# A fused decode backward kernel: outer products in two-row-group pieces under a scheduled TensorE order, in place of four-row-group units in a written order

## The chip, the cores and the metric

The kernel runs on one core of one Trainium2 chip. The metric is the time of one execution on the device, in microseconds. Three runs of the kernel before took 589.41, 590.72 and 583.35 us; their median is 589.41 us. The engines are named as in the profile: PE (TensorE, matmuls), PEld (TensorE's weight loads), DVE (VectorE), ACT (ScalarE), POOL (GpSimd, which also issues the store transfers), SP (SyncE, which issues the load transfers).

## The reference

One token for each of two batch entries passes a layer norm, and the normed row feeds two branches whose outputs are added to the input: attention over a cache, and a gated MLP. The kernel computes the output and the gradients of everything but a second, unused input.

```python
xn  = layernorm(x)                                   # x: 2 x 1 x 576, bf16
q   = (xn @ wq).reshape(2, 1, 32, 128)               # 32 query heads, 16 cache heads
s   = einsum(q, k_cache) * 128 ** -0.5               # caches: 2 x 16 x 4096 x 128
p   = softmax(s);  o = einsum(p, v_cache)            # two query heads share a cache head
out = x + o.reshape(2, 1, 4096) @ wo + ((xn @ w_gate) * (xn @ w_up)) @ w_down   # width 4608
grads = vjp(out)(grad_out)   # of x, k_cache, v_cache, wq, wo, w_gate, w_up, w_down
```

The gradients of the two caches have the caches' size. Each is an outer product per cache head: a column of probabilities (or of score gradients) times a row of 128. So 92.48 MB are read and 92.48 MB are written.

## The kernel before

**Iterations.** The 16 cache heads form 4 groups of 4. An iteration takes one group, one batch entry and two heads: 16 iterations (`NIT`), four to a group. In each, two K heads and two V heads (1 MB each, `head_load`) come in on SP's queue.

**Scores.** `head_scores` (L499 to L514) turns half a head with DVE transposes of 32 x 32 blocks (L104, tile X) and multiplies it with a stationary tile W in 16 matmuls of 128 columns (L510), summed in one PSUM tile ps_sc. K heads give the scores, V heads the gradients of the probabilities. It is a generator: it stops after eight matmuls, so that other work can be put between.

**Softmax.** `softmax_units` (L569 to L608) gives three pieces, called in steps j = 4, 5 and 6 of the iteration, among the V scores. `dscores` (L610) makes the score gradients in the next iteration. `masked` (L540) lets GpSimd spread rows with a mask into prm and dsm, the left operands of the outer products.

**Contractions.** `contract` (L516, 64 matmuls of 32 columns of weights) multiplies the rows with V (for the output) at j = 0 of the next iteration, and with K (for the gradient of q) at j = 2; `select` follows one step later. Until then the heads hold their slots in the ring `nat` of 12 slots, which also holds the weights wq, wo (of a group) and wgu, wd (of an MLP slice).

**Outer products.** `outer_units` (L547) gives four units for two heads. A unit takes both PSUM buffers ps_o, of two banks each, and fills them with 16 matmuls in which the row group a runs fastest:

```python
o = [ps_o(), ps_o()]
for c in range(4):
    for a in range(4):
        nc.tensor.matmul(o[a // 2][:, a % 2, c * Dh:(c + 1) * Dh],
                         lhsT=rows[32 * a:32 * a + 32, 4 * ch + c, :], ...)
```

Then `evac` (L86) copies each buffer to a store tile of 8 KB a partition; it picks ACT (L95) or DVE (L92) by a planned load of the two, which it adds up while the program is written. After two units GpSimd issues the store of the whole head (L564, 1 MB). The store tiles come from a ring `st` of five. The MLP's and the weights' gradients (`outer_gu`, `outer_down`, `outer_tail`, `outer_q`, `outer_qt`, `outer_o`) have the same form; in the last group the tiles of wq's and wo's gradients come from `nat`.

**Order.** TensorE's instructions stay in the order in which they are written (`manual_schedule`, L83); the other engines' order is found by the scheduler. The main loop (L812 to L886) has eight steps j an iteration: eight score matmuls, one outer unit (`more`), eight score matmuls, then pieces of the previous iteration's contractions, of the softmax, and of `side`, the list of other work (`other`). An MLP slice (one of nine, 512 wide, `mlp_units`) is loaded at j = 3 of iterations 0, 1, 2, 4, 6, 8, 10 and 12 and its ten units join `side` at the next iteration; slice 0 is there at the start. The next group's weights are loaded at the third iteration of a group. After the last iteration one more round of the loop issues the eight outer units that are left, and behind it come the last group's `back_units` and the final rows.

Of the kernel before, what the change touches and what calls it, by code (L numbers as in the profile page):

```python
# [13 lines left out]
P = 128  # L14
# [9 lines left out]
def kernel(  # L24
# [30 lines left out]
    G = 4  # L55
# [26 lines left out]

    ctx.enter_context(tc.manual_schedule(engines={mybir.EngineType.PE}))  # L83
# [178 lines left out]
    def dxn(stat, weight, pos, koff, kstep, half):  # L262


        Wm, Wt = stat
        X = xtile([P, 9, FS // 2], "Xw")
        t32(view(pairs(X[:].rearrange("p c n -> p (c n)")), 0, P, 0, [[1, 9 * P]]),
            view(pairs(weight[:].rearrange("p c n -> p (c n)")), 0, P, P * half, [[2 * P, 9], [1, P]]))
        dve(1.4)
        dp = ps_m([P, 160])  # L270
        for r in range(4):
            for gq in range(4):
                q, s = 2 * half + gq // 2, 4 * (gq % 2) + r
                nc.tensor.matmul(  # L274
                    dp[32 * gq:32 * gq + 32, 0:P], lhsT=view(Wm[:], 0, P, 8 * pos(q, s), [[1, 32]]),
                    rhs=view(X[:], 0, P, koff(s) * 256 + (2 * (q % 2) + (s // 2) % 2) * 64 + s % 2,
                             [[kstep * 256, 4], [2, 32]]),
                    start=(r == 0), stop=(r == 3))
        for r in range(2):
            for gq in range(4):  # L280
                q, s = 2 * half + gq // 2, 2 * (gq % 2) + r
                nc.tensor.matmul(
                    dp[32 * gq:32 * gq + 32, P:160], lhsT=view(Wt[:], 0, P, 8 * (4 * q + s), [[1, 32]]),
                    rhs=view(X[:], 0, P, 8 * 256 + (2 * (q % 2) + s // 2) * 64 + s % 2, [[2, 32]]),
                    start=(r == 0), stop=(r == 1))
        nc.vector.tensor_add(accx[:], accx[:], dp[:])
        dve(0.35)


    def mlp_units(i):  # L290
# [62 lines left out]
        def back(half):  # L353
            return lambda: dxn(m["W"], m["wgu"], lambda q, s: q * 8 + s, lambda s: (s // 4) * 4, 1, half)

        def outer_gu(w):
            def f():
                hb = m["hb"]
                st = swtile([P, 4, FS], "stw")
                o = [ps_o(), ps_o()]  # L360
                for dc in range(4):
                    for a in range(4):
                        nc.tensor.matmul(o[a // 2][:, a % 2, dc * P:(dc + 1) * P],
                                         lhsT=xnr[32 * a:32 * a + 32, dc * P:(dc + 1) * P],
                                         rhs=hb[32 * a:32 * a + 32, 1 + w, :], start=True, stop=True)
                for A in range(2):
                    evac(view(st[:], 0, P, 256 * A, [[P, 2], [FS, 4], [1, P]]),
                         o[A][:].rearrange("p a (d f) -> p a d f", d=4), 1024)
                out = (out_6, out_7)[w]
                nc.gpsimd.dma_start(out[0:512, f0:f0 + FS].rearrange("(c p) n -> p c n", p=P), st[:])  # L370
            return f

        def outer_tail():
            hb = m["hb"]
            st = tailtile("stt")
            o = [ps_o(), ps_o()]
            for w in range(2):
                for a in range(4):
                    nc.tensor.matmul(o[a // 2][64 * w:64 * w + 64, a % 2, 0:P], lhsT=xnr[32 * a:32 * a + 32, 512:576],
                                     rhs=hb[32 * a:32 * a + 32, 1 + w, :], start=True, stop=True)  # L380
            for A in range(2):
                evac(st[:, 256 * A:256 * A + 256].rearrange("p (a f) -> p a f", a=2), o[A][:, :, 0:P], 256)
            for w, out in enumerate((out_6, out_7)):
                nc.gpsimd.dma_start(out[512:576, f0:f0 + FS], st[64 * w:64 * w + 64])

        def outer_down(k):
            def f():
                hb = m["hb"]
                if k == 0:
                    m["sd"] = swtile([P, FC, D], "std")  # L390
                st = m["sd"]
                o = [ps_o(), ps_o()]
                for a in range(4):
                    nc.tensor.matmul(o[a // 2][:, a % 2, 0:HD2], lhsT=hb[32 * a:32 * a + 32, 0, :],  # L394
                                     rhs=dyr[32 * a:32 * a + 32, k * HD2:(k + 1) * HD2], start=True, stop=True)
                for A in range(2):
                    evac(st[:, 2 * A:2 * A + 2, k * HD2:(k + 1) * HD2], o[A][:, :, 0:HD2], D)
                if k == 1:
                    nc.gpsimd.dma_start(out_8[f0:f0 + FS, :].rearrange("(a p) n -> p a n", p=P), st[:])
            return f  # L400

        loads()
        return [gate_up, down, grads, outer_down(0), outer_down(1), back(0), back(1), outer_gu(0), outer_gu(1), outer_tail]


# [12 lines left out]
    def front_units(g, wq, wo):  # L418
        qd = sb.tile([P, 3, GH, 2], BF16, tag="qd", bufs=2, name="qd")
        rep = sb.tile([P, 2, 4, GH * 2], BF16, tag="rep", bufs=2, name="rep")  # L420

        def query():
            qp = ps_m([P, GH, 2])
            for h in range(GH):
                for dc in range(5):
                    if dc < 4:
                        l, r = wq[:, 2 * dc + h // 4, (h % 4) * P:(h % 4 + 1) * P], xs[:, dc, 0:2]
                    else:
                        l, r = wq[:, 8, (h % 4) * P:(h % 4 + 1) * P], xs[:, 4 + h // 4, 0:2]
                    nc.tensor.matmul(qp[:, h, :], lhsT=l, rhs=r, start=(dc == 0), stop=(dc == 4))  # L430
            nc.vector.tensor_copy(qd[:, 0], qp[:])
            nc.vector.tensor_scalar(qd[:, 2], qd[:, 0], SCALE, None, op0=ALU.mult)

        def grad(half):
            def f():
                Xo = xtile([P, GH // 2, D], "Xo")
                t32(pairs(Xo[:].rearrange("p c n -> p (c n)")),
                    pairs(wo[:, 4 * half:4 * half + 4].rearrange("p c n -> p (c n)")))
                do_ps = ps_m([P, P])
                for k in range(NB):  # L440
                    for e in range(2):
                        nc.tensor.matmul(
                            do_ps[:], lhsT=Wdy[:, k, e, :], rhs=view(Xo[:], 0, P, 64 * k + e, [[D, 4], [2, 32]]),
                            start=(k == 0 and e == 0), stop=(k == NB - 1 and e == 1),
                        )
                dof = sb.tile([P, GH // 2, 32], FP32, tag="dof", bufs=2, name="dof")
                t32(dof[:].rearrange("p c n -> p (c n)"), do_ps[:])
                nc.vector.tensor_copy(qd[:, 1, 4 * half:4 * half + 4], dof[:, :, 0:2])
                dve(2.0)
            return f  # L450

        def spread(t):

            def f():
                rp = ps_m([P, 4, GH * 2])
                for be in range(4):
                    nc.tensor.matmul(rp[:, be, :], lhsT=sel[:, be].rearrange("p a i -> p (a i)"),
                                     rhs=qd[:, t].rearrange("p h b -> p (h b)"), start=True, stop=True)
                nc.vector.tensor_copy(rep[:, t], rp[:])
            return f  # L460

        st = dict(g=g, wq=wq, wo=wo, qd=qd, rep=rep, oT=oTs[g % 2])
        return st, [query, grad(0), spread(0), grad(1), spread(1)]
# [35 lines left out]
    def head_scores(n, t, x, s_ps, half):  # L499
# [5 lines left out]
        for e in range(2):  # L505
            if e == 1:
                yield
# [8 lines left out]
    def contract(rowsT, heads):  # L516
# [13 lines left out]
        o_sb = sb.tile([P, Dh], FP32, tag="o_sb", bufs=2, name="o_sb")  # L530
        nc.scalar.copy(o_sb[:], o_ps[:])
        act(0.3)
        return o_sb

    def select(o_sb):
# [11 lines left out]
    def outer_units(rows, bd, b, l0, oview):  # L547
        m = {}

        def unit(x, ch):  # L550
            def f():
                if ch == 0:
                    m["st"] = stile([P, 4, 8, Dh], "so")
                st = m["st"]
                o = [ps_o(), ps_o()]
                for c in range(4):
                    for a in range(4):
                        nc.tensor.matmul(o[a // 2][:, a % 2, c * Dh:(c + 1) * Dh],  # L558
                                         lhsT=rows[32 * a:32 * a + 32, 4 * ch + c, :],
                                         rhs=bd[32 * a:32 * a + 32, x * Dh:(x + 1) * Dh], start=True, stop=True)  # L560
                for A in range(2):
                    evac(st[:, 2 * A:2 * A + 2, 4 * ch:4 * ch + 4, :].rearrange("p a c d -> p a (c d)"), o[A][:], 1024)
                if ch == 1:
# [3 lines left out]
        return [unit(x, ch) for x in range(2) for ch in range(2)]  # L567

    def softmax_units(s_ps, r):  # L569
        def largest():  # L570
            mx = small("mx")
            nc.vector.reduce_max(mx[:], s_ps[:], axis=AX.X)
            mT = ps_m([1, P])
            nc.tensor.transpose(mT[:], mx[:], identf[:])
            m4 = small("m4", (1, 4))
# [230 lines left out]
    for f in front:  # L806
        f()
# [112 lines left out]
```

## Time and profile before

| | |
|---|---|
| profiled execution, its own time | 589.41 us |
| its span, first to last instruction | 587.6 us |
| mean granted TensorE clock | 0.745 |
| read and written | 92.48 MB each, 315 GB/s over the span |
| loads (SP's queue) and stores (GpSimd's queue), share of the 16 DMA engines' span | 42.8% and 41.9% |
| one eviction of a ps_o buffer, 128 x 1024, on ACT / on DVE | 1.015 / 1.220 us |
| one X transpose on DVE | 1.230 us |
| one mask on GpSimd | 1.888 us |
| store of one head, issue to landing (median) | 7.7 us |
| load of one K / V head, issue to landing (median) | 9.0 / 9.5 us |

In a group's row, "out<-in xcount" is followed by the group's busy time in us and the mean of one in ns, then by the idle time of the engine just before them and what ended most of it. A row of waits reads: engine, what it wrote, what it waited for, the line of that; us in total, times, the longest. PEclk is the share of full speed that TensorE's clock was granted. Matmuls are pipelined, so one matmul's duration includes the way through the array, and the distance between starts tells the rate.

### The profile page before, as it was taken

To read this page: it belongs to the slowest core of one execution; us is meant where nothing else is said; L and a number is where in the kernel's file an instruction comes from. 1 tells how busy PE (TensorE), PEld (TensorE's weight loads), DVE (VectorE), ACT (ScalarE), POOL (GpSimd) and SP (SyncE) were. 2 spreads that over 40 slices of the span, in tenths; PEclk is the share of its full clock that TensorE was granted. 3 is DMA by queue.
4 is the path that set the end of the run, shared out by engine and by line. 5 is a ranking of instruction groups with operands and counts; after the bars stand their busy time and mean duration, and the time that the engine had idled before them with its cause. 6 is when DMAs were issued, how large, how long until landed. Compare 5 with 4: busy or idle time off the path is not lost. (4 is left out here: it accounts for less than half of the span.)

```text
span 587.6 us, 20030 instructions
## 1 busy us (share of the span) xinstructions
PE 447.7 (76%) x8921; PEld 351.1 (60%) x8921; DVE 360.5 (61%) x636; ACT 332.1 (57%) x454; POOL 204.5 (35%) x372
## 2 busy tenths in 40 slices
PE   0677897696787888887888878877887878878763
PEld 0576675474666666666666656666676656656630
DVE  8685543565465555667665656567665646679555
ACT  1036666464575655665665756655666756676644
POOL 5115242141242342524242442524242443442412
PEclk9987757676677558769876667779878677799655
DMA  8985969779589799997989899897979899975554
GB/s 269 387 304 188 358 237 392 288 264 364 209 280 394 291 327 405 335 410 290 365 280 407 327 333 395 317 402 265 375 270 405 343 363 398 327 306 214 217 218 162
DMA packets 52911, 186.26 MB, mean 317 GB/s; under 512 B 4140, under 2 KB 19128, under 8 KB 44632
## 3 DMA queue, kind: packets, MB, share of 16 engines
q1 hardware_dynamic: 28392, 92.49, 42.8%
q0 software_dynamic: 24432, 92.48, 41.9%
q8 instruction: 70, 1.15, 0.8%
q14 instruction: 17, 0.14, 0.1%
HBM read 92.48 MB, written 92.48 MB: 315 GB/s over the span
## 5 line engine op out<-in xcount | busy, mean ns | idle before, releaser
L95 ACT CAST so<-ps_o 128x1024 bf16<-128x1024 f32 x232 | 224.6, 1015 | 152.7 <-PE ps_o L558 97.5
L104 DVE STREAM_TRANSPOSE X<-kv 128x1024 f32<-128x1024 f32 x128 | 156.5, 1230 | 100.0 <-PE ps_sc L510 56.4
L510 PE MATMUL ps_sc<-X,W 128*128 128x128 bf16 x2048 | 205.9, 259 | 11.3 <-DVE X L104 11.3
L510 PEld LDWEIGHTS <-W 128*128 128x128 bf16 x2048 | 155.6, 114 | 41.3 <-issue 29.7
L564 POOL DMA_DIRECT2D out_dram<-so x64 | 49.4, 772 | 90.7 <-ACT so L95 61.3
L558 PE MATMUL ps_o<-bd,prm 32*128 32x128 bf16 x1024 | 36.7, 252 | 32.3 <-ACT stw L95 13.0
L558 PE MATMUL ps_o<-bd,dsm 32*128 32x128 bf16 x1024 | 40.3, 265 | 11.8 <-ACT so L95 7.6
L558 PEld LDWEIGHTS <-prm 32*128 32x128 bf16 x1024 | 21.7, 105 | 43.9 <-issue 29.3
L525 PE MATMUL ps_m<-kv,rowT 128*32 128x128 bf16 x2048 | 47.1, 264 | 0.0
L543 POOL TENSOR_TENSOR dsm<-ds,maskc 128x1024 bf16<-128x1024 bf16 x16 | 30.2, 1888 | 34.0 <-DVE ds L622 34.0
L525 PEld LDWEIGHTS <-rowT 128*32 128x32 bf16 x2048 | 40.2, 120 | 3.0 <-issue 2.4
L479 POOL COPY dM<-qd 128x128 bf16<-128x128 bf16 x32 | 9.2, 289 | 92.9 <-PE ps_m L485 81.6
L92 DVE CAST so<-ps_o 128x1024 bf16<-128x1024 f32 x24 | 29.3, 1220 | 19.8 <-PE ps_o L558 17.5
L558 PEld LDWEIGHTS <-dsm 32*128 32x128 bf16 x1024 | 22.9, 110 | 25.3 <-issue 21.3
L472 POOL COPY W<-rep 32x16 bf16<-32x16 bf16 x128 | 24.6, 192 | 36.7 <-PE ps_sc L510 26.8
L543 POOL TENSOR_TENSOR prm<-pr,maskc 128x1024 bf16<-128x1024 bf16 x16 | 30.2, 1888 | 20.5 <-DVE pr L600 20.5
L95 ACT CAST stw<-ps_o 128x1024 bf16<-128x1024 f32 x29 | 28.2, 1015 | 9.0 <-ACT so L95 4.2
L104 DVE STREAM_TRANSPOSE Xw<-wgu 128x1152 f32<-128x1152 f32 x18 | 24.7, 1370 | 9.9 <-PE ps_sc L510 9.9
L370 POOL DMA_DIRECT2D out_dram<-stw x18 | 13.7, 760 | 37.1 <-ACT stw L95 21.1
L95 ACT CAST sto<-ps_o 128x576 bf16<-128x576 f32 x27 | 16.7, 645 | 14.1 <-PE ps_o L705 12.6
L95 ACT CAST std<-ps_o 128x576 bf16<-128x576 f32 x35 | 21.7, 659 | 3.4 <-PE ps_o L394 3.4
L257 POOL COPY Wt<-Wm 64x128 bf16<-64x128 bf16 x26 | 7.4, 285 | 40.4 <-DVE mr L578 24.3
(179 smaller groups left out, 577.7 us busy)
## 6 DMA issues: line engine op xcount, KB each, us to landing
out_dram<-so POOLq DMA_DIRECT2D x64, 1024.0 KB, 7.7
kv<-in_A_k_cache_dram SPq DMA_DIRECT2D x32, 1024.0 KB, 9.0
kv<-in_A_v_cache_dram SPq DMA_DIRECT2D x32, 1024.0 KB, 9.5
out_dram<-stw POOLq DMA_DIRECT2D x18, 512.0 KB, 9.4
wd<-in_B_w_down_dram SPq DMA_DIRECT2D x9, 576.0 KB, 6.1
out_dram<-std POOLq DMA_DIRECT2D x9, 576.0 KB, 4.8
wo<-in_A_wo_dram SPq DMA_DIRECT2D x4, 1152.0 KB, 15.2
wgu<-in_B_w_gate_dram SPq DMA_DIRECT2D x9, 512.0 KB, 7.2
```

The costliest lines, as they stand in the source:

```text
L92: nc.vector.tensor_copy(out=out, in_=in_)
L95: nc.scalar.copy(out, in_)
L104: nc.vector.transpose(out, in_)
L257: nc.gpsimd.tensor_copy(view(Wt[:], 64 * h, 64, 0, [[P // n, n], [1, P // n]]), view(Wm[:], 64 * h, 64, off, dims))
L370: nc.gpsimd.dma_start(out[0:512, f0:f0 + FS].rearrange("(c p) n -> p c n", p=P), st[:])
L472: nc.gpsimd.tensor_copy(view(W[t][:], 32 * a, 32, 28 + 32 * a, [[2 * WW, 4], [WW + 2, 2], [1, 2]]), view(st["rep"][:], 32 * a, 32, t * 4 * ...
L479: nc.gpsimd.tensor_copy(view(dM[:], 0, P, t * 2 * P, [[P + 2, 2], [4, 32], [1, 2]]), view(st["qd"][:], 0, P, (2 if t == 0 else 1) * GH * 2 ...
L510: nc.tensor.matmul(s_ps[:], lhsT=view(W[t][:], 0, P, (be * 2 + x) * WW + 28 - 4 * c8, [[1, P]]), rhs=view(X[:], 0, P, c8 * 64 + e, [[8 * 6 ...
L525: nc.tensor.matmul(o_ps[32 * cg:32 * cg + 32, :], lhsT=view(rowsT[:], 0, P, c4 * 32 + 4 * c8, [[1, 32]]), rhs=head[:, 8 * c4 + c8, :], sta ...
L543: nc.gpsimd.tensor_tensor(m[:], view(rows[:], 0, P, 0, [[0, 8], [1, P]]), view(maskc[:], 0, P, 0, [[1, 8], [0, P]]), ALU.mult)
L558: nc.tensor.matmul(o[a // 2][:, a % 2, c * Dh:(c + 1) * Dh], lhsT=rows[32 * a:32 * a + 32, 4 * ch + c, :], rhs=bd[32 * a:32 * a + 32, x * ...
L564: nc.gpsimd.dma_start(oview[b, :, :, l0 + x].rearrange("a m n -> m a n"), st[:].rearrange("p a c d -> p a (c d)"))
```

## The change

It does the following:

- `manual_schedule` goes: the scheduler finds TensorE's order too.
- Every outer product is cut in two pieces. A piece takes one ps_o buffer and two of the four row groups: eight matmuls, one eviction. `more` issues two pieces where it issued one unit. A store tile is still filled by four evictions, and a store still covers one head.
- The pieces of the softmax, of the front part of a group and of `contract` / `select` become one function each, called in one go. K scores, softmax, V scores and `dscores` lie in one iteration. V is contracted at its end; K is contracted in the middle of the next iteration's first head.
- `side` is a list of lists of pieces; `other` issues a list at a time, as many as leave it empty after four head slots. An MLP slice joins whenever fewer than five entries are left, its loads first. By the built program slices lie in iterations 0 to 8.
- The next group's weights are loaded at the fourth iteration of a group, not at the third.
- All tiles of gradients come from the ring `st`, in the last group too; `o_sb` and `dof` have one buffer in place of two.
- After the loop, outer pieces and back part are issued in turn, the final rows ahead of the last weights' gradients.

The core of the diff:

```diff
-    ctx.enter_context(tc.manual_schedule(engines={mybir.EngineType.PE}))
...
     def head_scores(n, t, x, s_ps, half):
...
         for e in range(2):
-            if e == 1:
-                yield
...
-        o_sb = sb.tile([P, Dh], FP32, tag="o_sb", bufs=2, name="o_sb")
+        o_sb = sb.tile([P, Dh], FP32, tag="o_sb", bufs=1, name="o_sb")
...
-        def unit(x, ch):
+        def unit(x, ch, A):
             def f():
-                if ch == 0:
+                if ch == 0 and A == 0:
                     m["st"] = stile([P, 4, 8, Dh], "so")
                 st = m["st"]
-                o = [ps_o(), ps_o()]
+                o = ps_o()
                 for c in range(4):
-                    for a in range(4):
-                        nc.tensor.matmul(o[a // 2][:, a % 2, c * Dh:(c + 1) * Dh],
-                                         lhsT=rows[32 * a:32 * a + 32, 4 * ch + c, :],
+                    for aa in range(2):
+                        a = 2 * A + aa
+                        nc.tensor.matmul(o[:, aa, c * Dh:(c + 1) * Dh], lhsT=rows[32 * a:32 * a + 32, 4 * ch + c, :],
                                          rhs=bd[32 * a:32 * a + 32, x * Dh:(x + 1) * Dh], start=True, stop=True)
-                for A in range(2):
-                    evac(st[:, 2 * A:2 * A + 2, 4 * ch:4 * ch + 4, :].rearrange("p a c d -> p a (c d)"), o[A][:], 1024)
-                if ch == 1:
+                evac(st[:, 2 * A:2 * A + 2, 4 * ch:4 * ch + 4, :].rearrange("p a c d -> p a (c d)"), o[:], 1024)
+                if ch == 1 and A == 1:
                     nc.gpsimd.dma_start(oview[b, :, :, l0 + x].rearrange("a m n -> m a n"),
                                         st[:].rearrange("p a c d -> p a (c d)"))
             return f
-        return [unit(x, ch) for x in range(2) for ch in range(2)]
+        return [unit(x, ch, A) for x in range(2) for ch in range(2) for A in range(2)]
...
-        stq = nat if g == NGRP - 1 else swtile
...
-        loads()
-        return [gate_up, down, grads, outer_down(0), outer_down(1), back(0), back(1), outer_gu(0), outer_gu(1), outer_tail]
+        return [[loads], [gate_up, down], [grads, back], [outer_down(0, 0), outer_down(0, 1)], [outer_down(1, 0), outer_down(1, 1)],
+                [outer_gu(0, 0), outer_gu(0, 1)], [outer_gu(1, 0), outer_gu(1, 1)], [outer_tail]]
...
+    def slot(src, t, b, l, s_ps, per, mid=None):
+        n = head_load(src, b, l)
+        head_scores(n, t, l % 2, s_ps, 0)
+        more(2)
+        if mid:
+            mid()
+        head_scores(n, t, l % 2, s_ps, 1)
+        more(2)
+        other(per)
+        return n
...
+    for n in range(NIT):
+        g, b, s = step(n)
+        l0 = G * g + 2 * s
+        if len(side) < 5 and nslice < NFS:
+            side += mlp_units(nslice)
+            nslice += 1
+        per = max(1, -(-len(side) // 4))
+        new = n + 1 < NIT and step(n + 1)[0] != g
+        K, V = [], []
+        if new:
+            loaded = group_loads(g + 1)
+        s_ps = ps_sc()
+        for x in range(2):
+            K.append(slot(kview, 0, b, l0 + x, s_ps, per, (lambda: end_of_K(*last[:5])) if x == 0 and last else None))
...
+        pr, pT, ex, rz = softmax(s_ps)
+        prm = masked(pr, "prm")
...
+        for x in range(2):
+            V.append(slot(vview, 1, b, l0 + x, dp_ps, per))
+            if x == 0:
+                outs += outer_units(prm, bd1, b, l0, ovview)
...
+        ds, dsT = dscores(pr, ex, rz, dp_ps)
+        dsm = masked(ds, "dsm")
+        end_of_V(st, b, s, V, pT)
...
+    side += final[:1] + units[:2] + final[1:] + units[2:]
     while outs or side:
-        more()
-        other(2)
+        more(2)
+        other(1)
```

## The prediction

> **What bounds the kernel now.** I read the stage table first, then the order of work on TensorE, then the waits, then the chain that ended last. The page's totals:
>
> ```profile
> span 587.6 us, 20030 instructions
> PE 447.7 (76%) x8921; PEld 351.1 (60%) x8921; DVE 360.5 (61%) x636; ACT 332.1 (57%) x454; POOL 204.5 (35%) x372
> ...
> L104 DVE STREAM_TRANSPOSE X<-kv 128x1024 f32<-128x1024 f32 x128 | 156.5, 1230 | 100.0 <-PE ps_sc L510 56.4
> L510 PE MATMUL ps_sc<-X,W 128*128 128x128 bf16 x2048 | 205.9, 259 | 11.3 <-DVE X L104 11.3
> ...
> L558 PE MATMUL ps_o<-bd,prm 32*128 32x128 bf16 x1024 | 36.7, 252 | 32.3 <-ACT stw L95 13.0
> L558 PE MATMUL ps_o<-bd,dsm 32*128 32x128 bf16 x1024 | 40.3, 265 | 11.8 <-ACT so L95 7.6
> ```
>
> No engine is full. The table by stretches shows two that take turns: TensorE and the transfers.
>
> ```profile
> core 0: us, PE busy (x) PEld busy (x) DVE busy (x) ACT busy (x) POOL busy (x), PEclk, DMA share, GB/s
> 36.00:184.00 148.00, 113.13 (x2238) 90.05 (x2235) 79.39 (x138) 85.94 (x120) 47.71 (x85) 0.72 0.80 288
> 184.00:416.00 232.00, 190.75 (x3834) 150.88 (x3834) 143.99 (x250) 139.28 (x192) 84.64 (x151) 0.73 0.93 347
> 416.00:538.00 122.00, 98.50 (x2066) 77.11 (x2065) 81.17 (x137) 79.48 (x110) 47.89 (x85) 0.80 0.89 338
> 538.00:587.60 49.60, 29.95 (x550) 19.12 (x547) 28.70 (x50) 25.09 (x33) 13.76 (x17) 0.59 0.53 198
> ```
>
> From 36 to 538 us TensorE is busy for 402 of 502 us, at three quarters of its clock, and the DMA engines for 80 to 93%. The timeline of TensorE shows what a block costs at each clock:
>
> ```profile
> 123.21 1.03 PE L510 MATMUL ps_sc<-X,W 128*128 128x128 bf16 x8
> 124.18 0.40 PE L558 MATMUL ps_o<-bd,prm 32*128 32x128 bf16 x16
> 124.52 0.63 PE L510 MATMUL ps_sc<-X,W 128*128 128x128 bf16 x8
> ...
> 134.99 1.01 PE L510 MATMUL ps_sc<-X,W 128*128 128x128 bf16 x8 [3.53 <-DVE X L104]
> 135.94 0.61 PE L558 MATMUL ps_o<-bd,prm 32*128 32x128 bf16 x16
> 136.48 0.39 PE L510 MATMUL ps_sc<-X,W 128*128 128x128 bf16 x2
> ```
>
> A full-height matmul of 128 columns starts every 58 ns at full clock and every 107 ns at half. Sixteen matmuls of 32 rows end after 0.40 and 0.61 us: four passes of 58 or 107 ns plus one matmul's own 0.22 or 0.28 us. So the four row groups run at once. From the start of the 16 to the next score matmul is 0.54 us at half clock where four passes are 0.43: a change of tile shape costs about 0.1 us.
>
> The clock goes by stretches of 3.41 us. I summed, in each, columns times the share of the array's height and width that each matmul holds. All 28 rises from half clock follow a stretch with at least 0.74 of what half clock can do; the fullest without a rise has 0.72. All 29 falls follow a full-clock stretch with at most 0.36; the emptiest without one has 0.37. Half clock is left only where TensorE is dense.
>
> The waits name who holds TensorE up:
>
> ```profile
> PE ps_o L558 <- ACT stw L95: 13.6, 23, 0.7
> PE ps_sc L510 <- DVE X L104: 11.3, 4, 5.0
> PE ps_o L558 <- ACT so L95: 8.8, 13, 1.1
> PE ps_o L363 <- ACT so L95: 8.3, 16, 0.7
> ```
>
> All its rows that wait for a ps_o buffer to be drained sum to 67 us. DVE's transposes of X wait 43.3 us for cache transfers (32.6 on V, 10.7 on K).
>
> **The change part by part.** The operations are the same; order, grouping and buffer lives change.
>
> *Row groups.* A unit was 16 matmuls over both ps_o buffers, four row groups at once; now it is two pieces of eight, each on two row groups. In the built order 99 of the 128 cache units keep their pieces side by side (the last pass of one overlaps the first of the next: 7 passes for 4), 29 do not (8 for 4): 99 x 3 + 29 x 4 = 413 more passes. At the mean clock of 0.745 a pass is 72 ns: 30 us. By the same count the MLP's gate and up units add 4 us, the down, wo and wq units (288 and 256 columns, 162 and 143 ns a pass) about 6. Together 40 us of TensorE, 32 if all at full clock, 58 at half. Against it, a piece needs one drained buffer, not two, so much of the 67 us of waits goes under it. I put half, 20 us, on the path; ends 0 (all hidden) and 58.
>
> *Changes of shape.* The scheduler now picks TensorE's order and cuts scores and contractions into smaller runs: 683 changes of tile shape in the built program for 522. 161 x 0.1 = 16 us, half on the path: 8; ends 0 and 21 (0.13 each).
>
> *Clock.* Scores 8, outer 16 at half clock: 0.86 + 0.43 + 0.2 for two changes of shape; the array's share is 1.28 of 1.48 us = 0.86. Now scores 16, outer 8 and 8: 1.71 + 0.80 + 0.2 and 2.13 of 2.71 = 0.79; where the scheduler cuts finer (8, 8, 8, 8) it is 0.72. The margin over 0.73 halves, so rises come later. One point of mean clock is worth 402 x 0.01 / 0.745 = 5.4 us. I take two points, 11 us; ends: three points up (fewer waits), -16, and ten down, +55. The Trainium skill, TensorE: Matmul & The Clock Gate, Part 1, says that about 3.4 us of sustained activity raises the clock and an idle window of that length lowers it. Here most of the 29 falls come without such idleness, so the measured share decides; by the page's rule the clock term would be nothing and the sum 11 us lower.
>
> *Where the MLP goes.* Row maxima (L572) start once an iteration, so their distances time it: with a slice in three neighbouring iterations 37.5, 40.4, 41.5 us; with a lone slice 31.8, 33.2, 33.8, 32.6, 30.8; without any 26.9, 26.7 and, last, 20.8. A slice costs 13.0 in a row and 5.6 alone. The new loop adds one whenever under five units are left: slices fall in iterations 0 to 8, none after. Five lone slices join the row: 5 x 7.4 = +37 at most. Six late intervals without one may run at 20.8 for 26.8, as less is in flight: -36 at best, but their 8.4 MB each at the 347 GB/s of the table is 24 us. I take half of that -18 with 28 of the 37, since the group's own weights keep interfering: +10; ends -36 and +37.
>
> *Buffers.* K is contracted half a cache slot earlier and wq, wo of the next group are loaded one iteration later, so slots of the 12-deep ring come free earlier; SP's queue waited 73.0 us on contractions. That can take at most the 43.3 us of DMA waits off; most now lie where the clock, not the data, will pace. A slice's five loads move on SP's queue from ahead of the previous iteration's V loads to behind the first K load of their own, just before gate and up read them; up lands in 10.4 us, a K head in 9.0, so at worst TensorE waits 9 x 1.4 = 13 us more. I take -8; ends -43 and +13. What is late next is TensorE itself.
>
> *Tail.* From the last dscores (546.9) to the end are 40.7 us: eight units, then the group's back part.
>
> ```profile
> 559.90 0.62 PE ps_o L558 x14
> ...
> 560.55 1.02 ACT so L95
> ...
> 561.61 0.75 PE ps_o L558 x15
> ```
>
> Matmuls and evictions alternate at 1.8 us a unit. Six units are left instead of eight (-3.6), and the back part is issued among them; against it the last stores share the five-tile ring. -6; ends -12 and +4. SP's and POOL's issues keep their number; the final rows' 7 us of DVE work (L760 to L798), until now behind outer_o's first two units, stand ahead of all of them, where ACT's evictions cover it.
>
> *At nothing.* Store ring: all waits of ACT and DVE on landings of stores sum to under 6 us, and a tile is still filled by four evictions of 1.0 us. One o_sb and one dof buffer: their readers end microseconds before the next writer. GpSimd masks stay at 1.89 us, behind 16 or more matmuls; if that cover goes, each shows up to 2 us as a wait of ps_o on prm (8.3 us now).
>
> Sum: 20 + 8 + 11 + 10 - 8 - 6 = +35 us. The profiled execution took 589.4 us (span 587.6, 1.8 around it) and is itself the median of the three: **624 us**.
>
> **The rivals.** *Faster: TensorE better fed.* Earlier buffers and single ps_o pieces keep it dense in iterations 0 to 8, the clock rises. Without its clock term the sum is +24, so from 4.4 points up (0.79) it breaks even; at 0.83 it is 24 - 46 = -22: 567 us. For it: 67 + 43 us of waits to win; the stretch 513 to 547 held full clock. Against it: the same matmuls fill less of the array per pass.
>
> *Half clock settles in.* The MLP part stays below 0.73, ten points lost: 24 + 55 = +79, 668 us. For it: 107 to 124 us stayed at half clock while TensorE was busy 15 of 17 us.
>
> *No change that shows.* From 184 to 416 us the DMA share is 0.93; if transfers pace there and the added passes lie in TensorE's 67 + 11 us of waits, only the small terms remain: 590 us. Against it: DMA share 0.80 before 184 us.
>
> **How the numbers follow.** Forecast (604 to 650 of its own) 0.52; half clock 0.20; no change 0.14; better fed 0.14. A measurement of this kernel tells about 2% from no change (577.6 to 601.2). Better fed is nearly all faster (0.13); no change and the rest of it give 0.15; the others are slower, 0.72. The range leaves out the outer part of both extreme rivals: 565 to 668.
>
> **What would show it.** Two-row groups: ps_o matmuls on bd near 55 us each for 36.7 and 40.3. Clock: mean granted clock near 0.72. MLP: distances of row maxima near 42 us up to iteration 8, then 21 to 27. Tail: from the last ds to the end about 35 us. Buffers: DVE's waits on cache transfers under 43 us. I am wrong if ps_o's matmul time does not grow, if the clock stays at or above 0.79, or if the late iterations save more than the early ones lose.

## The result, and the profile after

The changed kernel took 554.59 us, the median of four runs (551.08 to 561.93), where the kernel before took 589.9 (583.35 to 590.72). The ratio is 0.940, with a 95% interval of 0.931 to 0.950: 35 us faster. Forecast were 624 us, 35 us slower, and the range began at 565, so the sign was wrong and the range too high. The profiled execution is the longest of the four (561.93 us at a mean clock of 0.766; the others had 0.777 to 0.797), so its rows show rather too little of the gain. A run that is over 1.5% slower than the fastest of its kernel, as this one is, is left out of the ratios here and below, so a ratio can differ by some thousandths from that of the medians.

The page of the kernel after, its totals and the groups that answer to those shown of before:

```profile
span 560.2 us, 20059 instructions
PE 475.7 (85%) x8921; PEld 362.5 (65%) x8921; DVE 362.0 (65%) x624; ACT 330.6 (59%) x454; POOL 204.6 (37%) x372
...
L503 PE MATMUL ps_sc<-X,W 128*128 128x128 bf16 x2048 | 197.2, 249 | 5.3 <-DVE X L102 4.5
L102 DVE STREAM_TRANSPOSE X<-kv 128x1024 f32<-128x1024 f32 x128 | 157.6, 1233 | 44.1 <-PE ps_sc L503 42.7
...
L549 PE MATMUL ps_o<-bd,dsm 32*128 32x128 bf16 x1024 | 50.9, 245 | 10.3 <-ACT so L93 5.8
...
L549 PE MATMUL ps_o<-bd,prm 32*128 32x128 bf16 x1024 | 46.3, 250 | 14.3 <-POOL prm L533 7.0
```

TensorE is busy for 28 us more than before (475.7 for 447.7) in a span that is 27 us shorter. The outer products on bd take longer, 97.2 us for 77.0; the experiments below show that this comes with the new order and hardly with the pieces. DVE's transposes wait 44.1 us for 100.0, and nearly all of that is for TensorE (42.7): the 43.3 us that they waited on cache transfers are gone altogether.

The table by stretches of the kernel after (its columns are those of the table before):

```profile
36.00:184.00 148.00, 131.53 (x2656) 102.77 (x2654) 96.33 (x170) 97.25 (x137) 57.29 (x104) 0.82 0.93 351
184.00:416.00 232.00, 210.22 (x3875) 161.59 (x3873) 149.36 (x245) 143.96 (x199) 87.01 (x153) 0.73 0.95 359
416.00:510.00 94.00, 85.16 (x1548) 64.68 (x1547) 57.84 (x99) 56.50 (x77) 35.84 (x67) 0.73 0.80 308
510.00:560.20 50.20, 33.61 (x607) 20.60 (x604) 30.18 (x53) 26.73 (x34) 13.79 (x17) 0.70 0.53 195
```

The gain begins in the first row. From 36 to 184 us TensorE is busy for 131.5 us where it was 113.1, at a clock of 0.82 for 0.72, and the DMA engines for 0.93 where they were 0.80: 2656 matmuls are done there for 2238. From 36 us to the last 50, TensorE is busy for 427 of 474 us (90%), before for 402 of 502 (80%).

The waits of TensorE for a drained ps_o buffer, which summed to 67.7 us, now sum to 28.3. The largest rows of all of TensorE's waits behind the start of the kernel after:

```profile
PE ps_o L549 <- ACT so L93: 11.7, 27, 0.8
PE ps_o L549 <- POOL prm L533: 7.0, 6, 1.4
PE ps_sc L503 <- DVE X L102: 4.5, 10, 0.7
```

### The profile page after: what moved, and what is told of

The parts are those of the page before. It is cut to its first block, busy times and chain, and to the rows that moved or that the text cites. A ratio compares the mean times of both kernels' runs of the same rounds, so it can differ in the third digit from the quotient of the medians.

```text
span 560.2 us, 20059 instructions
## 1 busy us (share of the span) xinstructions
PE 475.7 (85%) x8921; PEld 362.5 (65%) x8921; DVE 362.0 (65%) x624; ACT 330.6 (59%) x454; POOL 204.6 (37%) x372
## 4 chain that ended last, share of the span: by engine, by line
PE 31%; ACT 9%; issue 5%; DVE 4%; POOL 2%; POOLq 0%; DVEq 0%; ACTq 0%
PE ps_sc L503 11%; ACT so L93 8%; PE ps_o L549 6%; PE ps_m L518 4%; PE ps_m L527 1%; POOL prm L533 1%; PE ps_m L440 1%; PE ps_o L681 1%; DVE so L90 1%; PE ps_o L651 1%; DVE sto L90 1%; PE ps_m L272 1%; PE ps_o L364 1%; PE ps_m L618 1%; DVE X L102 1%
## 5 line engine op out<-in xcount | busy, mean ns | idle before, releaser
L503 PE MATMUL ps_sc<-X,W 128*128 128x128 bf16 x2048 | 197.2, 249 | 5.3 <-DVE X L102 4.5
L102 DVE STREAM_TRANSPOSE X<-kv 128x1024 f32<-128x1024 f32 x128 | 157.6, 1233 | 44.1 <-PE ps_sc L503 42.7
L503 PEld LDWEIGHTS <-W 128*128 128x128 bf16 x2048 | 153.1, 112 | 27.7 <-issue 17.5
L549 PE MATMUL ps_o<-bd,dsm 32*128 32x128 bf16 x1024 | 50.9, 245 | 10.3 <-ACT so L93 5.8
L518 PE MATMUL ps_m<-kv,rowT 128*32 128x128 bf16 x2048 | 59.3, 272 | 0.0
L549 PE MATMUL ps_o<-bd,prm 32*128 32x128 bf16 x1024 | 46.3, 250 | 14.3 <-POOL prm L533 7.0
L518 PEld LDWEIGHTS <-rowT 128*32 128x32 bf16 x2048 | 43.0, 121 | 10.0 <-issue 5.8
L549 PEld LDWEIGHTS <-dsm 32*128 32x128 bf16 x1024 | 30.4, 104 | 24.8 <-issue 18.4
L549 PEld LDWEIGHTS <-prm 32*128 32x128 bf16 x1024 | 27.8, 105 | 26.8 <-issue 13.5
L719 DVE TENSOR_SCALAR oT<-ps_m 128x4 bf16<-128x4 f32 x16 | 2.7, 171 | 29.6 <-PE ps_m L527 29.6
## 6 DMA issues: line engine op xcount, KB each, us to landing
kv<-in_A_k_cache_dram SPq DMA_DIRECT2D x32, 1024.0 KB, 11.8
wo<-in_A_wo_dram SPq DMA_DIRECT2D x4, 1152.0 KB, 13.4
```

The lines of the kernel that those rows point to most:

```text
L102: nc.vector.transpose(out, in_)
L503: nc.tensor.matmul(s_ps[:], lhsT=view(W[t][:], 0, P, (be * 2 + x) * WW + 28 - 4 * c8, [[1, P]]), rhs=view(X[:], 0, P, c8 * 64 + e, [[8 * 6 ...
L518: nc.tensor.matmul(o_ps[32 * cg:32 * cg + 32, :], lhsT=view(rowsT[:], 0, P, c4 * 32 + 4 * c8, [[1, 32]]), rhs=head[:, 8 * c4 + c8, :], sta ...
L549: nc.tensor.matmul(o[:, aa, c * Dh:(c + 1) * Dh], lhsT=rows[32 * a:32 * a + 32, 4 * ch + c, :], rhs=bd[32 * a:32 * a + 32, x * Dh:(x + 1) ...
```

## The experiments

Four parts of the change could have made the gain: TensorE's order, now found by the scheduler; the place of the loads on SP's queue; the pieces that take one ps_o buffer; the softmax and contractions called in one go. For the first four experiments (the order alone, the pieces alone, both loads moved, whole units put back) the theory on record was the loads and the slots of the ring that they take; rival 1 was the order, rival 2 the pieces. When they had shown both the order and the loads to gain, the theory of the next four was that these two add. Ratios are to the kernel before, run on the same chip beside each experiment, with 95% intervals; differences in time are taken from the ratios, times 588 us.

**The scheduler's order alone, on the old loop.** Before, with one line less:

```diff
-    ctx.enter_context(tc.manual_schedule(engines={mybir.EngineType.PE}))
```

> The kernel before with only the written order of TensorE taken away. Theory (loads and ring slots: the heads arrive in time because slots come free earlier and the weights are asked for later): this edit moves neither, so DVE's waits on cache transfers stay near 43 us and the time stays within 10 us of 590. Rival 1 (the scheduler's order of TensorE makes the gain): most of the 35 us appear, 555 to 570 us. Rival 2 (pieces): nothing here, 580 to 600.

Measured: 559.66 us for 587.22, ratio 0.952 (0.945 to 0.959), 28 us less. This is rival 1's range; the theory, within 10 us of 590, missed. The mean clock rose to 0.786, and waits for a drained ps_o fell from 67.7 to 29.5 us with the units still whole. One spot of TensorE's timeline shows why. Before, two gradients of wq, eight matmuls each, with the eviction between them:

```profile
208.41 0.61 PE L675 MATMUL ps_o<-R,xnr 32*128 32x256 bf16 x8
210.16 0.82 PE L675 MATMUL ps_o<-R,xnr 32*128 32x256 bf16 x8 [1.14 <-ACT stq L95]
210.92 1.03 PE L510 MATMUL ps_sc<-X,W 128*128 128x128 bf16 x8
```

The second group waits 1.14 us for ScalarE, and the scores behind it wait too, though all they need is there. It is so nearly throughout: before has 113 such waits, and in 101 of them (59.0 of the 67.7 us) the transposed tile of the next score matmul was complete when the wait began. The same units under the scheduler's order (the timeline of the experiment):

```profile
195.96 0.39 PE L673 MATMUL ps_o<-R,xnr 32*128 32x256 bf16 x4
196.29 0.23 PE L508 MATMUL ps_sc<-X,W 128*128 128x128 bf16 x1
196.45 0.39 PE L673 MATMUL ps_o<-R,xnr 32*128 32x256 bf16 x4
196.78 0.23 PE L508 MATMUL ps_sc<-X,W 128*128 128x128 bf16 x1
...
197.04 0.62 PE L508 MATMUL ps_sc<-X,W 128*128 128x128 bf16 x8
```

Scores go between while a buffer is not drained. These are the cuts that the prediction charged as changes of shape; they are what fills the waits. They have a price too: the scheduler's order runs 98 times only eight matmuls on bd in a row, where before runs sixteen 124 times out of 125, and with the same units of four row groups their busy time rises from 77.0 to 98.8 us:

```profile
L556 PE MATMUL ps_o<-bd,prm 32*128 32x128 bf16 x1024 | 48.2, 246 | 18.9 <-DVE stw L90 6.4
L556 PE MATMUL ps_o<-bd,dsm 32*128 32x128 bf16 x1024 | 50.6, 248 | 10.2 <-ACT sto L93 7.4
```

What this kernel leaves as it was is seen in the waits of its DVE on cache transfers, 44.1 us in all (43.3 before):

```profile
DVE X L102 <- DMA kv<-in_A_v_cache_dram: 35.3, 7, 7.0
...
DVE X L102 <- DMA kv<-in_A_k_cache_dram: 8.8, 5, 2.4
```

**The written order in the new loop.** After, with that line put back:

```diff
+    ctx.enter_context(tc.manual_schedule(engines={mybir.EngineType.PE}))
```

> The changed kernel with TensorE's order as written (the removed line put back). Theory now (two causes that add: the scheduler's order fills TensorE's waits of 0.5 to 2 us, and the later loads free the ring): only the loads' part is left, 570 to 585 us, TensorE's gaps of 0.5 to 2 us back at 55 us or more. Rival (the new main loop's written order is itself the better one): 550 to 562 us.

Measured: 660.39 us for 585.71, ratio 1.130 (1.122 to 1.138), about 111 us above the kernel after and far outside both ranges. TensorE's gaps of 0.5 to 2 us are back, as the theory said, but at 90.0 us (55 or more expected). Three rows of its waits:

```profile
PE ps_m L570 <- DVE mr L568: 25.5, 16, 2.6
PE ps_m L529 <- ACT o_sb L526: 15.9, 31, 1.2
...
PE ps_m L577 <- ACT ex L575: 12.1, 16, 1.0
```

These are links of the softmax and of `select`, which now stand in one go; in the written order TensorE waits at each of them, 53.5 us in these rows where after has 7.7. Its waits for a drained ps_o are at 66.5 us again (28.3 in after). So the new loop in a written order is a loss; only with the scheduler's order is the whole a gain.

**The pieces alone.** Before, in `unit`:

```diff
-                o = [ps_o(), ps_o()]
-                for c in range(4):
-                    for a in range(4):
+                for A in range(2):
+                    o = ps_o()
+                    for c in range(4):
+                        for a in (2 * A, 2 * A + 1):
```

with one eviction behind each A.

> The kernel before with only the cache's outer products cut into pieces on one ps_o buffer and two row groups each; TensorE's order stays written. Theory (loads and ring): the added passes show, 20 us of TensorE as in the changed kernel's trace, 590 to 605 us, and DVE's waits on cache transfers stay near 43 us. Rival 2 (a piece that needs one drained buffer keeps TensorE fed): 560 to 580 us, and the waits of ps_o on evictions fall from 67 to under 30 us. Rival 1 (order): 590 to 605.

Measured: 586.44 us for 587.22, ratio 1.001 (0.997 to 1.005), no difference, and in none of the three ranges. Waits for a drained ps_o fell from 67.7 to 56.9 us. The busy time on bd rose by only 4.4 us, to 81.4:

```profile
L559 PE MATMUL ps_o<-bd,prm 32*128 32x128 bf16 x1024 | 39.6, 246 | 28.7 <-ACT stw L95 11.4
...
L559 PE MATMUL ps_o<-bd,dsm 32*128 32x128 bf16 x1024 | 41.8, 267 | 5.7 <-ACT so L95 2.1
```

The starts in the trace say why. Passes on one row group start 56 ns or more apart at full clock, but in a unit of two pieces a second pair of matmuls starts 27 ns (median) after the first pair: it is that of the second piece, on the other two row groups, and the two pieces run beside each other. From the first of the sixteen to the next score matmul it is 0.355 us at full clock and 0.567 at half, where whole units take 0.335 and 0.547 (medians): 20 ns more.

**Both loads moved, on the old loop.** `mlp_units` returns its loads, the loop issues them behind the first K load of the slice's own iteration, and the group's weights come one iteration later:

```diff
+                    if j == 0 and ld:
+                        ld()
+                        ld = None
...
-            if n % 4 == 2 and g + 1 < NGRP:
+            if n % 4 == 3 and g + 1 < NGRP:
```

> The kernel before with only the loads moved as in the change: an MLP slice's five loads behind the first K load of the iteration that uses them, the next group's weights in the group's fourth iteration instead of the third. Theory (loads and ring): DVE's waits on cache transfers fall from 43 to under 20 us, the DMA share between 36 and 184 us rises from 0.80 to 0.88 or more, 565 to 578 us. Rivals 1 and 2: no change, 583 to 595 us.

Measured: 572.86 us for 587.22, ratio 0.976 (0.970 to 0.982), 14 us less. DVE's waits on cache transfers fall from 43.3 to 3.1 us, and the DMA share from 36 to 184 us rises from 0.80 to 0.87 (0.88 or more was expected).

**The slices' loads alone (first edit), and the group's loads alone (second edit).**

> The kernel before with only the MLP slices' loads moved (behind the first K load of the iteration that uses them). It parts the 14 us that both moves of loads gave. Theory a (a slice's 1.8 MB lying early in the ring is what keeps K and V out, nine times): 572 to 578 us. Theory b (the group's 2.3 MB held one iteration longer, three times, is what counts): 583 to 589 us.

> The kernel before with only the next group's weights loaded in the group's fourth iteration in place of the third. Theory a: 583 to 589 us. Theory b: 572 to 578 us.

Measured, both against 589.54 us: the slices' loads 571.28 us, ratio 0.969 (0.965 to 0.974); the group's loads 587.96, ratio 0.996 (0.993 to 1.000). It is the five loads of a slice (571.28 lies just under theory a's range); that both moves together gave 14 us and these alone 18 lies within the intervals. In the kernel before, SP's own waits show them standing on its queue until a slot of the ring is free:

```profile
SPq L297 <- PE ps_m L348: 49.3, 6, 15.1
SPq L300 <- DVE Xw L104: 37.9, 4, 10.7
```

With their smaller rows these loads wait 116.3 us, and SP issues one load after the other, so the next V and K heads stand behind them. For five of the slices (loaded at 160, 229, 289, 360 and 421 us) the last load waits 8 to 11 us, and both V heads behind it go out within 3 us of it. With the slices' loads moved the same rows sum to 20.4 us. SP's waits in all fall only from 518 to 478 us: it waits for heads' slots instead. A slice loaded early does two things at once, it stands ahead on the queue and it takes slots of the ring; no experiment parts the two. What DVE still waits for on transfers in that experiment (for 43.3 us before):

```profile
DVE X L104 <- DMA kv<-in_A_k_cache_dram: 6.2, 2, 3.2
```

With the group's loads alone moved they stay at 16.3 + 16.1 us, and the gain of 2 us lies at the edge of its interval.

**The loads put back, in the new loop.** After, with a slice's loads behind the second K load of the iteration ahead and the group's loads an iteration earlier:

```diff
-        if new:
+        if n % 4 == 2 and g + 1 < NGRP:
             loaded = group_loads(g + 1)
...
+        if nslice < NFS:
+            ld, *units = mlp_units(nslice)
+            ld()
```

> The changed kernel with the loads where the kernel before has them: an MLP slice's ahead of the previous iteration's V loads, the next group's weights in the group's third iteration. Theory (two causes that add): 8 to 16 us slower than the changed kernel, 563 to 571 us, and DVE waits for cache transfers again, 15 us or more. Rival (with the scheduler's order the place of the loads no longer matters): 550 to 560 us.

Measured: 560.34 us for 585.71, ratio 0.958 (0.948 to 0.967), about 10 us worse than after; the two intervals just overlap, and the median lies between the two expected ranges. SP waits 121.4 us on the slices' loads again (13.4 in after), and DVE 15.1 us on cache transfers (none in after). The price points the same way as on the old loop, 10 us for 14.

**Both gains on the old loop.** Before with the line removed and both loads moved, nothing else:

```diff
-    ctx.enter_context(tc.manual_schedule(engines={mybir.EngineType.PE}))
...
+                        ld()
...
+            if n % 4 == 3 and g + 1 < NGRP:
```

> The kernel before with two edits alone: the scheduler's order for TensorE, and the loads moved as in the change. Theory (two causes that add): 590 - 28 - 14 = 548 us, 542 to 554, as fast as or faster than the changed kernel, with the row groups still four. Rival (the two overlap: both remove the same waits): 555 to 562 us.

Measured: 540.9 us for 585.71, ratio 0.926 (0.919 to 0.934), 43 us less and a little under the theory's range. The product of the two single ratios is 0.952 x 0.976 = 0.929, so they add. These two edits make more than the whole change does: the rest of the change costs some 8 us. The intervals (0.919 to 0.934 and 0.931 to 0.950) just overlap.

**What costs the rest: the slices in a row, and the pieces.** After, with slices put where before had them; after, with whole units of 16 matmuls again over two buffers, one for each `more`; and after with both:

```diff
-        if len(side) < 5 and nslice < NFS:
+        if n in (1, 2, 3, 5, 7, 9, 11, 13):
```

```diff
-                o = ps_o()
+                o = [ps_o(), ps_o()]
...
+                    for a in range(4):
...
-        more(2)
+        more(1)
```

> The changed kernel with MLP slices in iterations 0, 1, 2, 3, 5, 7, 9, 11 and 13, as the kernel before works on them, in place of 0 to 8. The prediction's step (a slice in neighbouring iterations costs more than a lone one, +10 net): 540 to 550 us. Rival (bunching costs nothing once the ring feeds): 552 to 560 us. Second rival (late iterations without slices run with less in flight, so spreading them costs): 560 to 570 us.

> The changed kernel with the cache's outer products put back to units of 16 matmuls over both ps_o buffers and four row groups. Theory (loads and ring): the gain stays and the 20 us of added passes go again from TensorE, 540 to 556 us; ps_o matmuls on bd take about 77 us in place of 97. Rival 2 (pieces make the gain): 575 to 592 us. Rival 1 (order): 545 to 560.

> The changed kernel with four row groups a unit and the slices spread as before. If the two losses inside the change (8 us by the row groups, 6 by the bunched slices) add: 539 to 543 us, the time of the kernel before with the scheduler's order and the moved loads alone. If they overlap (both act through the clock): 543 to 548 us.

Measured: slices spread 548.34 us, ratio 0.932 (0.922 to 0.942); whole units 546.35, 0.928 (0.919 to 0.937); both 543.67, 0.923 (0.918 to 0.929). So about 5, 7 and 10 us better than after (by the medians 6, 8 and 11); each single interval still overlaps that of after (0.931 to 0.950), the one of both does not. The two single gains overlap, as 543.67 us against the expected 539 to 543 (they add) or 543 to 548 (they overlap) says too, but only just. The 546.35 us lie in the range of the theory and of rival 1 alike, and the expectation missed in one point: their matmuls did not go back to 77 us. The groups of that experiment:

```profile
L548 PE MATMUL ps_o<-bd,dsm 32*128 32x128 bf16 x1024 | 50.4, 232 | 10.0 <-ACT so L93 4.1 <-issue 1.5 <-DVE so L90 1.4
...
L548 PE MATMUL ps_o<-bd,prm 32*128 32x128 bf16 x1024 | 43.4, 242 | 10.5 <-ACT so L93 4.6 <-POOL prm L533 4.2 <-issue 0.5
```

93.8 us, against 97.2 in after: here too the unit of 16 is often pulled apart, with 93 runs of eight and 61 of sixteen. So the 7 us cannot be put down to saved passes; its clock is higher (0.806 to 0.830 in the runs counted, 0.777 to 0.797 in those of after), and what raised it stays open.

**K contracted later.** After, with K's contraction in the second head of the next iteration, half a cache slot later:

```diff
-            K.append(slot(kview, 0, b, l0 + x, s_ps, per, (lambda: end_of_K(*last[:5])) if x == 0 and last else None))
+            K.append(slot(kview, 0, b, l0 + x, s_ps, per, (lambda: end_of_K(*last[:5])) if x == 1 and last else None))
```

> The changed kernel with K contracted in the middle of the next iteration's second head in place of its first, about where the kernel before does it. The prediction's step (earlier release of two K slots is worth up to 43 us with the loads, taken as 8): 558 to 566 us and DVE waits for cache transfers. Rival (the loads' place alone frees enough): 551 to 557 us.

Measured: 559.76 us for 589.54, ratio 0.950 (0.946 to 0.954), about 6 us worse than after with intervals that just overlap. The waits of DVE on cache transfers that were expected did not come: there are none. So that the earlier release of the two K slots is worth these 6 us is not shown.

**Where TensorE's idle time went.** From the trace's records of matmuls I took the gaps between one's end and the next one's start, from 36 us to 45 us ahead of the last matmul's end. In us, with the number of gaps:

| kernel | idle | in gaps over 2 us | in gaps of 0.5 to 2 us |
|---|---|---|---|
| before | 99.6 | 14.9 (5) | 65.0 (77) |
| pieces alone | 94.1 | 16.4 (5) | 60.1 (73) |
| both loads moved | 85.0 | 9.6 (4) | 56.3 (72) |
| scheduler's order alone | 57.2 | 19.9 (7) | 26.9 (25) |
| order and both loads, old loop | 47.3 | 18.1 (6) | 16.2 (17) |
| after | 47.2 | 2.1 (1) | 28.1 (39) |
| after with whole units | 51.6 | 2.5 (1) | 31.9 (39) |
| after, written order | 134.2 | 14.4 (6) | 90.0 (120) |

The scheduler's order takes the short gaps and leaves the long ones. The moved loads take some of both (5 and 9 us), and with both edits the long gaps are still there, so the length of the gaps does not part the two gains. The waits do: the order takes those for a drained ps_o (67.7 to 29.5 us) and leaves DVE's on cache transfers at 44.1; the loads take the latter (43.3 to 3.1) and leave 60.0 of the former; both edits together take both, to 20.1 and 11.8.

## Why the prediction was wrong, point by point

**The step that failed: changes of shape (+8 us), as the price of TensorE's new order.** The prediction read the scheduler's order as cuts that cost 0.1 us each. It did see the 67 us of waits for ps_o, but set only the pieces' single buffer against them. On the chip the pieces take 11 us of these waits and no time (ratio 1.001); the order takes 38 us of them and 28 us of time, although TensorE's shape changes 785 times in its trace where before has 544. The rows for it stood in the profile of before: TensorE waiting for an eviction 113 times, 69 of them 0.5 us or longer, nearly always with score matmuls behind it whose transposed tile was complete. Of an engine that keeps a written order this has to be asked at every wait: is there work behind it that is ready?

**Row groups: +20 on the path. This step failed too, in its count of passes.** For pieces that stay side by side the prediction counted seven passes where a unit has four, as if the second piece began under the last pass of the first. It begins some 27 ns after the first does, beside it: 20 ns more a unit, where three passes at the mean clock were 216. The pieces alone cost 4.4 us of busy time and no time. That ps_o's rows grew in after (50.9 and 46.3, near 55 each forecast) is a coincidence of numbers: whole units under the scheduler's order show 50.6 and 48.2. A run of eight alone holds TensorE for 0.33 us at full clock, as long as sixteen do, and the order makes many of them. In the new loop whole units are better by 7 us, but not through this time.

**Buffers and loads: -8, wrong in size and in cause.** The prediction expected earlier slots from the contractions and the group's loads, and priced the move of a slice's loads as a risk of up to 13 us. It was the other way round: that move alone is worth 18 us, the group's loads 2, K's contraction perhaps 6. The range's end of 43 us was there, but the mechanism was overlooked: a load that waits on SP's queue, or that takes a slot early, holds up the heads behind it. The prediction counted what the moved load may lose, not what the loads that go ahead of it win.

**Clock: two points down, +11. The sign was wrong.** The profiled execution shows 0.766 for 0.745, two points up, and the others 0.777 to 0.797; the scheduler's order alone 0.786, the written order in the new loop 0.706. The share per block (0.86 to 0.79) was argued for a TensorE that is never idle, and with pieces that run one behind the other. That the clock followed the gaps that went is likely but not shown: with whole units in the new loop TensorE is idle for 51.6 us, more than in after, at a higher clock.

**Where the MLP goes: +10.** About +5 measured, with intervals that overlap. The distances of row maxima up to iteration 9 were 25.4 us and then 30.6 to 43.4, only three of them above 40 where all were expected near 42; five of the six late ones were 22.6 to 25.0, in the stated 21 to 27, and one 39.5. The 13.0 us for a slice in a row may have contained the wait for the loads, which is now gone; no run shows that apart.

**Tail: -6.** From the last dscores to the end it is 36.4 us for 40.7: -4.2. Right.

**At nothing.** Waits on landings of stores stay small: those of ACT and DVE on a store tile are 0.3 us for 4.8. GpSimd's masks show 7.0 us as a wait of ps_o on prm, 8.3 before. Right.

**The rival that came true** is the one that ended on the other side, TensorE better fed, at 0.14. It broke even at a clock of 0.79; the runs stood at 0.766 to 0.797 and went further, for its +24 was too high by the same missing term. It came true by luck in part: of the causes it names, the single ps_o pieces do nothing alone, and it does not name the order. The new sum, from runs: the order and the loads together -43 on the old loop, the rest of the change +8: -35, as measured. Of the +8, slices in a row and whole units given up are +10 together and the tail -4; these small parts overlap and are not shown one by one.

Open remain: why whole units are some 7 us better though their matmuls take nearly as long, what raised the clock there, and whether K's earlier contraction is worth its 6 us.

## What to carry to other kernels

Where an engine runs in a written order, look at each of its frequent waits for work behind it that is ready: many waits of half a microsecond to one are a sum that an order found by the scheduler can take, and cuts into smaller runs are its price, not its result. On a load queue that is worked off in order, issue a load that waits for a buffer behind those that are needed sooner. When several parts are changed at once, measure the parts alone: here two edits make 0.926 and the whole change only 0.940.

## What was not expected of the hardware

**The clock counts the filled part of the array, in the kernel after too.** Summed as in the prediction, with each matmul in the stretch of 3.41 us in which it starts and from 32 us on, the 23 rises from half clock follow a stretch with at least 0.75 of what half clock can do (128 columns in 107 ns), and the fullest without a rise has just under 0.75; the 24 falls follow one with at most 0.34 of twice that, and the emptiest full-clock stretch without a fall has 0.35. The same count in before gives 0.71 and 0.75 for the rises, 0.35 and 0.36 for the falls, so the border of the rises is sharp to a few hundredths only. Busy time without the weight by height and width does not separate them: in after there are half-clock stretches with TensorE busy throughout and no rise, and a fall behind a stretch that is busy to 0.94. 23 of the falls lie between 36 and 515 us, where TensorE has one gap of over 2 us (2.1).

The Trainium skill, TensorE: Matmul & The Clock Gate, Part 1, lets the clock fall after an idle window of about 3.4 us; no such window is there in that stretch, and the clock falls 23 times, so the measured share holds.

**Two pieces side by side cost almost what one unit costs; a run of eight alone costs as much as sixteen.** Eight matmuls on two row groups and eight on the other two, one behind the other in TensorE's order, take 20 ns more than sixteen that go round all four (0.355 for 0.335 us to the next score matmul at full clock). Eight with scores behind them take 0.33 us. So what made the outer products dearer is where the order cuts, not how many row groups a piece is written for.
